# A transformer block on one core: the first layer norm in another order, with x tiles, row sums and scale weights rearranged

## The chip, the cores and the metric

The kernel runs on one core of one Trainium2 chip. The metric is device time in microseconds (us). Every run is of one core. Each run also has the granted clock of the matrix engine, averaged over the run. An average of 1.0 says that no window at a lower clock is on record. Two things escape it. The clock records of these traces begin only at 5.87 to 8.84 us, and the slow warm-up before that (a warm-up every 0.43 us, against 0.22 later) isn't counted. And a trace without any clock record also counts as 1.0.

Names used below: PE is the matrix engine and PEld its weight loads, DVE is VectorE, ACT is ScalarE, POOL is GpSimd, SP is the queue that issues the loads.

## The reference

```python
mod = silu(c) @ w_mod                       # six vectors of 1024: sa, ca, ga, sb, cb, gb
h = layernorm(x) * (1 + ca) + sa            # x: 2048 rows of 1024, bf16
x = x + ga * linear_attention(h)            # h @ wqkv, 32 heads, phi = elu + 1, then @ wo
h = layernorm(x) * (1 + cb) + sb
x = x + gb * swiglu(h)                      # F = 3584
```

Only the first two lines, for the first 512 rows, are touched by the change.

## The kernel before

x stands in tiles of 128 rows (`XRES[:, st, :]`), and four tiles make a chunk. For chunk 0 each tile is normalised, transposed on PE into PSUM (`ps` in the profiles, where its matmuls write), multiplied by the scale column `1 + ca` on its way to `HT`, and used by the first q matmuls. The scale and shift columns come from `w_mod`: `WCA` holds its scale part and `WSA` its shift part, and `mod_sc` makes columns of them with matmuls of one column. PE has nothing real to do before the first tile is normalised, so `warm` gives it matmuls on dummy data.

```python
for st in range(4):
    P.dma("x0_%d" % st, XRES[:, st, :], xv[:, st, :])
...
ca_load(0)            # scale columns 0-511, 1 MB
wq_load(0, 2)
ca_load(1)            # scale columns 512-1023
wq_load(2, 2)
wq_load(4, 2)
sa_load(1)            # shift columns 512-1023
wq_load(6)
wq_load(7)
sa_load(0)            # shift columns 0-511
... # (cut)
act_stats(2)                             # ACT: sum and sum of squares of tile 2
warm(13, bank=3)
s0_[0](); s0_[1](); s1_[0](); s0_[2]()   # DVE: bn_stats of tiles 0, 1; one statement a line in the kernel
ln1_rstd1(0)                             # POOL: (var + eps) ** -0.5
s1_[1](); s1_[2]()
ln1_rstd1(1)
ln1_xn(0)                                # DVE normalises tile 0
tile_transposes(0)
warm(5, bank=3)
s3_[0]()
ln1_xn_act(1)                            # ACT normalises tile 1
tile_transposes(1)
... # (cut: tile 2's mean and variance from ACT's sums, tile 3's bn_stats)
ln1_xn(2)
ln1_xn(3)
mod_sc(WCA, 8, range(2))
fin_ca(0, 2)
tile_transposes(2, 3)
h0_first(0, "dve")                       # PSUM * scale -> HT, then the first q matmuls
... # (cut)
# q phase, in PE's order: q parts dt 0, 1 | mod_sc(WCA, 4..7) | dt 2, 3 | dt 4 |
#   mod_sc(WSA, 6..7) | dt 4, 5 | ... | mod_sc(WSA, 0..3), the last shift columns | dt 7
```

Of the kernel before, what the change touches and what calls it, by code (L numbers as in the profile page):

```python
# [9 lines left out]
ALU = mybir.AluOpType  # L10
# [252 lines left out]
def bass_adaLN_cond__linear_attn_block__swiglu_ffn__prompt_kernel(  # L263
# [12 lines left out]
    S, D = A_x.shape[1], A_x.shape[2]  # L276
# [9 lines left out]
    with ExitStack() as es:  # L286
# [6 lines left out]
        def T(name, off, shape, dt):  # L293
            n = 1
            for s_ in shape[1:]:
                n *= s_
            assert off % 32 == 0 and off + n * mybir.dt.size(dt) <= ARENA, (name, off, shape)
            return nc.alloc_sbuf_tensor_at(name, shape, dt, offset=base + off)

        KB = 1024  # L300
        XRES = T("xres", 0, [128, NST, D], BF16)
        PQT = T("pqt", 32 * KB, [128, NHG, S], BF16)
        WCA = T("wca", 32 * KB, [128, NDT, D], BF16)
# [12 lines left out]
        MV = T("mv", SM + 1632, [128, NST, 2], FP32)  # L316
        VE = T("ve", SM + 1760, [128, NST], FP32)
        RSTD = T("rstd", SM + 1824, [128, NST], FP32)
        NEGHALF = T("neghalf", SM + 1888, [128, 4], FP32)
        SUMX = T("sumx", SM + 1920, [128, NST], FP32)  # L320
        SUMSQ = T("sumsq", SM + 1984, [128, NST], FP32)
# [68 lines left out]
        wmv = w_mod.rearrange("(kt p) n -> p kt n", p=128)  # L390
        cv8 = c.rearrange("o (kt p) -> (o kt) p", p=128)

        P = _Prog()

        P.dma("c", CS8[0:NDT, :], cv8, queue="act")
        for st in range(4):
            P.dma("x0_%d" % st, XRES[:, st, :], xv[:, st, :])

        def ca_load(p):
            P.dma("wca%d" % p, WCA[:, :, 512 * p:512 * p + 512], wmv[:, :, D + 512 * p:D + 512 * p + 512])  # L400

        def sa_load(p):
            P.dma("wsa%d" % p, WSA[:, :, 512 * p:512 * p + 512], wmv[:, :, 512 * p:512 * p + 512])

        def wq_load(i, n=1):
            P.dma("wq%d" % i, WQK[:, i:i + n, 0:D], wqkvv[:, i:i + n, 0:D])

        ca_load(0)
        wq_load(0, 2)
        ca_load(1)  # L410
        wq_load(2, 2)
        wq_load(4, 2)
        sa_load(1)
        wq_load(6)
# [36 lines left out]
        def warm(n=1, bank=2):  # L451
            for _ in range(n):
                P.pe("matmul", out=PS[:, bank, :], lhsT=IDENT[:], rhs=E1[:, 0, :], start=True, stop=True)
# [6 lines left out]
        def ln1_stats_ops(st):  # L460
            par, j = (st // 4) % 2, st % 4
            return [
                lambda: P.dve("bn_stats", out=STATS[:, par, j, 0, :], in_=XRES[:, st, 0:512]),
                lambda: P.dve("bn_stats", out=STATS[:, par, j, 1, :], in_=XRES[:, st, 512:1024]),
                lambda: P.dve("bn_aggr", out=MV[:, st, :], in_=STATS[:, par, j, :, :]),
            ]
# [10 lines left out]
        def ln1_xn(st):  # L477
            P.dve("tensor_scalar", out=XRES[:, st, :], in0=XRES[:, st, :],
                  scalar1=MV[:, st, 0:1], scalar2=RSTD[:, st:st + 1], op0=ALU.subtract, op1=ALU.mult)
# [22 lines left out]
        def mod_sc(w, c0, ms):  # L502
            for m in ms:
                for kt in range(NDT):
                    P.pe("matmul", out=PS[:, 0, c0 + m:c0 + m + 1], lhsT=w[:, kt, m * 128:(m + 1) * 128],
                         rhs=SILUC[:, kt:kt + 1], start=mod_first[0], stop=(kt == NDT - 1), skip_group_check=True)
                    mod_first[0] = False

        def fin_ca(m, n):
            P.dve("tensor_scalar", out=MODCOL[:, 0, m:m + n], in0=PS[:, 0, 8 + m:8 + m + n], scalar1=1.0, scalar2=None,  # L510
                  op0=ALU.add)
# [26 lines left out]
        def h0_first(dt, eng):  # L538
            if eng == "act":
                P.act("activation", out=HT[:, 0, dt, :], in_=t_view(dt), func=ACT.Copy, scale=MODCOL[:, 0, dt:dt + 1])  # L540
            else:
                P.dve("tensor_scalar", out=HT[:, 0, dt, :], in0=t_view(dt), scalar1=MODCOL[:, 0, dt:dt + 1],
                      scalar2=None, op0=ALU.mult)
# [12 lines left out]
        def ln1_rstd1(st):  # L556
            P.dve("tensor_scalar", out=VE[:, st:st + 1], in0=MV[:, st, 1:2], scalar1=EPS, scalar2=None, op0=ALU.add)
            P.pool("tensor_tensor", out=RSTD[:, st:st + 1], in0=VE[:, st:st + 1], in1=NEGHALF[:, 0:1], op=ALU.pow)

        def ln1_xn_act(st):  # L560
            P.dve("tensor_scalar", out=NMR[:, st:st + 1], in0=MV[:, st, 0:1], scalar1=RSTD[:, st:st + 1],
                  scalar2=-1.0, op0=ALU.mult, op1=ALU.mult)
            P.act("activation", out=XRES[:, st, :], in_=XRES[:, st, :],
                  func=ACT.Identity, scale=RSTD[:, st:st + 1], bias=NMR[:, st:st + 1])

        def ln1_rstd2(st):
            P.dve("tensor_scalar", out=VE[:, st:st + 2], in0=MV[:, st:st + 2, 1], scalar1=EPS, scalar2=None, op0=ALU.add)
            P.pool("tensor_tensor", out=RSTD[:, st:st + 2], in0=VE[:, st:st + 2], in1=NEGHALF[:, 0:2], op=ALU.pow)
# [3 lines left out]
        def act_stats(st, c0=0, mid=None):  # L572
            n = (D - c0) // 512
            junk0 = HT[:, 1, 0:2, :] if st < 8 else JUNK1
            for fn_, sc_, acc_ in ((ACT.Identity, 1.0 / D, SUMX), (ACT.Square, D ** -0.5, SUMSQ)):
                P.act("activation", out=junk0[:, 0:n, :], in_=XRES[:, st, c0:D].rearrange("p (a b) -> p a b", a=n),
                      func=fn_, scale=sc_, accum_out=acc_[:, st:st + 1])
                if mid is not None:
                    mid()
                    mid = None  # L580

        def act_mv_ops(st):
            return [
                lambda: P.dve("tensor_copy", out=MV[:, st, 0:1], in_=SUMX[:, st:st + 1]),
                lambda: P.dve("scalar_tensor_tensor", out=MV[:, st, 1:2], in0=SUMX[:, st:st + 1],
                              scalar=SUMX[:, st:st + 1], in1=SUMSQ[:, st:st + 1], op0=ALU.mult, op1=ALU.subtract),
            ]

        def neg_rstd(st):
            P.dve("tensor_scalar", out=VE[:, st:st + 1], in0=MV[:, st, 1:2], scalar1=-1.0, scalar2=EPS, op0=ALU.mult,  # L590
                  op1=ALU.add)
            P.pool("tensor_tensor", out=RSTD[:, st:st + 1], in0=VE[:, st:st + 1], in1=NEGHALF[:, 0:1], op=ALU.pow)

        act_stats(2)
        s0_, s1_, s3_ = ln1_stats_ops(0), ln1_stats_ops(1), ln1_stats_ops(3)
        m2 = act_mv_ops(2)

        def tile_transposes(*js):
            for dt in range(NDT):
                for j in js:  # L600
                    c = (dt % 2) * 512 + j * 128
                    P.pe("transpose", out=PSB[:, 4 + dt // 2, c:c + 128], in_=XRES[:, j, dt * 128:(dt + 1) * 128],
                         identity=IDENT[:])

        warm(13, bank=3)
        s0_[0]()
        s0_[1]()
        s1_[0]()
        s0_[2]()
        ln1_rstd1(0)  # L610
        s1_[1]()
        s1_[2]()
        ln1_rstd1(1)
        ln1_xn(0)
        tile_transposes(0)
        warm(5, bank=3)
        s3_[0]()
        ln1_xn_act(1)
        tile_transposes(1)
        warm(0, bank=3)  # L620
        m2[1]()
        m2[0]()
        neg_rstd(2)
        s3_[1]()
        s3_[2]()
        ln1_rstd1(3)
        ln1_xn(2)
        ln1_xn(3)
        mod_sc(WCA, 8, range(2))
        fin_ca(0, 2)  # L630
        tile_transposes(2, 3)
        h0_first(0, "dve")
        h0_first(1, "dve")
        raw_copy(4, "dve")
# [456 lines left out]
        for ch in range(NCH):  # L1091
# [34 lines left out]
            for j in range(4):  # L1126
                st = 4 * ch + j
# [61 lines left out]
```

## Time and profile before

| | before |
|---|---|
| time, median of 3 runs | 831.27 us (831.02 to 831.39) |
| profiled span | 829.4 us |
| PE busy | 824.2 us |
| first q matmul starts | 11.87 us |

The page of the profiled run, its first lines: busy time of each engine, with the share of the span.

```profile
span 829.4 us, 10016 instructions
PE 824.2 (99%) x4083; PEld 379.2 (46%) x4083; DVE 310.3 (37%) x665; ACT 196.3 (24%) x335; POOL 40.7 (5%) x58
```

PE is busy nearly all the time. Where it is not, the chain of waits tells. Columns: start, length, engine and tile (us).

```profile
0.79 2.74 DMA xres<-in_A_x_dram
...
3.55 1.88 DVE stats L176 x3
...
9.36 0.79 POOL rstd L176
...
10.17 0.56 DVE xres L176
...
10.78 1.01 PE ps L176 x15
...
11.87 114.85 PE ps L176 x673
...
145.30 0.76 DVE g L176
...
146.11 680.82 PE ps L176 x3229
...
826.95 0.30 DVE ut L176
```

Up to 11.87 us the chain is the norm; from there it is PE, but for a side path (cut here) that ends at 146.11, where PE waits for the z row (sums for the attention that go out to DRAM and come back). The timeline of the first 12 us (start, length, engine, instruction, count, and in brackets the idle time before it and what ended it):

```profile
2.61 5.62 PE L176 MATMUL ps<-e,ident 128*128 128x512 bf16 x13 [0.22 <-DVE e L176]
...
5.40 1.06 ACT L176 ACTIVATE ht<-xres 128x1024 bf16<-128x1024 bf16 x1 [2.53 <-DMA xres<-in_A_x_dram]
...
8.06 0.61 PE L176 MATMUL ps<-ident,xres 128*128 128x128 bf16 x8
...
8.51 1.24 PE L176 MATMUL ps<-e,ident 128*128 128x512 bf16 x5
...
9.59 0.61 PE L176 MATMUL ps<-ident,xres 128*128 128x128 bf16 x8
...
11.84 0.56 PEld L176 LDWEIGHTS ps<-ht,wqk 128*128 128x128 bf16 x4 [0.22 <-issue]
...
20.62 0.67 PEld L176 LDWEIGHTS ps<-siluc,wsa 128*128 128x128 bf16 x16
...
24.95 1.07 PEld L176 LDWEIGHTS ps<-siluc,wsa 128*128 128x128 bf16 x32
```

What to see: the 13 warm-ups run right into the first transposes (8.06), five more fill the time to the next (9.59), ACT stands idle until the third x tile lands (5.40), and the shift weights (`wsa`) are used at 20.62 and 24.95 without a wait. From issue and time to landing they land at 20.50 and 24.87, so there is 0.1 us to spare.

The stretches view, for the start and for three kinds of load. Columns: stretch and its length, busy time of PE, PEld, DVE, ACT and POOL with instruction counts, granted clock, DMA share, GB/s.

```profile
7.98:11.39 3.41, 3.29 (x50) 2.48 (x49) 2.45 (x10) 1.24 (x1) 1.33 (x2) 1.00 1.08 368
6.20:9.00 2.80, 2.80 (x17) 1.30 (x15) 2.70 (x11) 2.44 (x5) 1.60 (x3) 1.00 1.07 378
13.90:15.10 1.20, 1.20 (x8) 0.52 (x6) 0.54 (x2) 0.46 (x2) 0.00 (x0) 1.00 1.05 385
233.00:243.00 10.00, 10.00 (x48) 4.50 (x46) 4.79 (x17) 3.45 (x6) 4.72 (x6) 1.00 1.20 291
```

In all four the DMA share is over 1 (1.05 to 1.20). The last stretch is a burst of FFN weights in runs of 512 bytes (5678 of its 5770 packets), at 291 GB/s. The two before it carry runs of mostly 1 KB (693 of 882 packets, 378 GB/s) and of 2 KB (201 of 264, 385 GB/s).

### The profile page before, as it was taken

The numbers are of one execution on the slowest core, as the hardware profiler recorded it, in microseconds if no ns is written. First come the engines' busy times: TensorE is split into PE (matmuls) and PEld (weight loads), VectorE is DVE, ScalarE is ACT, GpSimd is POOL, SyncE is SP. The second block draws the span as 40 slices with busy tenths as digits, with TensorE's granted clock in tenths as the row PEclk, the third lists the DMA queues.
The fourth block names the chain that finished last, engine by engine and source line by source line (L and its number), as shares of the span: only waits on it lengthen the run. The fifth ranks groups of instructions, "written<-read, shape, count | busy, mean of one in ns | idle before, by whom it ended". The sixth has DMA issues, their size and how long they took to land.

```text
span 829.4 us, 10016 instructions
## 1 busy us (share of the span) xinstructions
PE 824.2 (99%) x4083; PEld 379.2 (46%) x4083; DVE 310.3 (37%) x665; ACT 196.3 (24%) x335; POOL 40.7 (5%) x58
## 2 busy tenths in 40 slices
PE   8999999999999999999999999999999999999998
PEld 4544444444444444444444444444444444444444
DVE  5797986666955521111221111122111111111111
ACT  3757641323242111011111101111110111111011
POOL 1010000000130000030000003000000300000000
PEclk9999999999999999999999999999999999999999
DMA  9969655938397985700455571045557004553000
GB/s 324 283 151 230 151 158 172 191 113 304 59 258 226 290 255 154 194 25 13 125 151 152 153 188 31 14 125 153 153 150 193 26 17 123 153 152 89 0 26 26
DMA packets 199246, 119.29 MB, mean 144 GB/s; under 512 B 57880, under 2 KB 182944, under 8 KB 199200
## 3 DMA queue, kind: packets, MB, share of 16 engines
q1 hardware_dynamic: 199184, 118.65, 52.7%
q8 instruction: 32, 0.52, 0.3%
q14 instruction: 14, 0.11, 0.0%
q10 hardware_dynamic: 16, 0.00, 0.0%
HBM read 100.67 MB, written 4.33 MB: 127 GB/s over the span
## 4 chain that ended last, share of the span: by engine, by line
PE 96%; DMA 2%; DVE 1%; SPq 0%; ACT 0%; issue 0%; POOL 0%; ACTq 0%
PE ps L176 96%; DMA z_row<-zr 1%; DMA zb<-z_row 0%; DVE stats L176 0%; DMA xres<-in_A_x_dram 0%; DVE mhl L176 0%; SPq L176 0%; DVE xres L176 0%; DVE pqt L176 0%; POOL rstd L176 0%; DVE g L176 0%; DVE mv L176 0%; ACT gtmp L176 0%; ACT e L176 0%; DVE ve L176 0%
## 5 line engine op out<-in xcount | busy, mean ns | idle before, releaser
L176 PE MATMUL ps<-h2t,gug 128*128 128x512 bf16 x896 | 211.7, 379 | 0.0
L176 PE MATMUL ps<-h2t,guu 128*128 128x512 bf16 x896 | 211.7, 379 | 0.0
L176 DVE TENSOR_TENSOR at<-sg,ps 128x512 bf16<-128x512 bf16 x112 | 77.0, 687 | 284.8 <-PE ps L176 283.2
L176 ACT ACTIVATE sg<-ps 128x512 bf16<-128x512 f32 x112 | 66.9, 597 | 309.7 <-PE ps L176 309.7
L176 PEld LDWEIGHTS ps<-h2t,guu 128*128 128x128 bf16 x896 | 87.7, 98 | 105.7
L176 PEld LDWEIGHTS ps<-h2t,gug 128*128 128x128 bf16 x896 | 87.6, 98 | 105.5
L176 PE MATMUL ps<-wd_a,at 128*128 128x512 bf16 (+2 forms) x528 | 113.5, 373 | 0.0
L176 PE MATMUL ps<-ht,wqk 128*128 128x512 bf16 x512 | 111.8, 379 | 0.1
L176 PE MATMUL ps<-wd_b,at 128*128 128x512 bf16 (+2 forms) x396 | 85.8, 373 | 0.0
L176 PEld LDWEIGHTS ps<-wd_a,at 128*128 128x128 bf16 x528 | 51.1, 98 | 59.8
L176 DVE TENSOR_TENSOR ut<-att,gb_b 128x512 bf16<-128x512 bf16 (+1 forms) x32 | 13.5, 421 | 167.7 <-ACT att L176 167.7
L176 PEld LDWEIGHTS ps<-ht,wqk 128*128 128x128 bf16 x512 | 49.4, 98 | 58.7 <-DVE ht L176 0.4
L176 ACT ACTIVATE att<-ps 128x512 bf16<-128x512 f32 (+1 forms) x32 | 17.4, 591 | 182.1 <-PE ps L176 182.1
L176 PEld LDWEIGHTS ps<-wd_b,at 128*128 128x128 bf16 x396 | 38.3, 98 | 44.7
L176 PE MATMUL ps<-pk,xres 128*128 128x512 bf16 x256 | 56.7, 379 | 0.1
L176 PE MATMUL ps<-mw,pqt 128*128 128x512 bf16 x256 | 56.3, 379 | 0.0
L176 POOL TENSOR_SCALAR h2t<-h2t,modcol 128x512 bf16<-128x512 bf16 x32 | 26.4, 841 | 383.1 <-DMA h2t<-xn 383.1
L176 ACT ACTIVATE e<-ps 128x512 bf16<-128x512 f32 x56 | 33.1, 603 | 31.8 <-PE ps L176 19.6
L176 PEld LDWEIGHTS ps<-mw,pqt 128*128 128x128 bf16 x256 | 24.9, 98 | 30.2 <-DVE xres L176 0.4
L176 PEld LDWEIGHTS ps<-pk,xres 128*128 128x128 bf16 x256 | 24.8, 98 | 30.3 <-DVE g L176 0.6
L176 ACT ACTIVATE junk<-xres 128x1024 bf16<-128x1024 bf16 x24 | 25.4, 1058 | 35.1 <-DVE xres L176 34.9
L176 DVE SCALAR_TENSOR_TENSOR xres<-ps,xres 128x512 bf16<-128x512 f32 x32 | 21.4, 688 | 12.3 <-PE ps L176 11.5
(102 smaller groups left out, 341.1 us busy)
## 6 DMA issues: line engine op xcount, KB each, us to landing
gug<-in_B_w_gate_dram SPq DMA_DIRECT2D x56, 512.0 KB, 4.0
guu<-in_B_w_up_dram SPq DMA_DIRECT2D x56, 512.0 KB, 5.3
xres<-in_A_x_dram SPq DMA_DIRECT2D x20, 256.0 KB, 7.7
rb<-recip_den SPq DMA_DIRECT2D x8, 512.0 KB, 12.1
stgx<-in_w_mod_dram SPq DMA_DIRECT2D x2, 2048.0 KB, 7.9
wd_a<-in_B_w_down_dram SPq DMA_DIRECT2D x4, 1024.0 KB, 7.4
out_dram<-xres SPq DMA_DIRECT2D x31, 128.0 KB, 1.7
xres<-in_A_x_dram SPq DMA_DIRECT2D x3, 1024.0 KB, 14.2
```

What stands on the lines that cost most here:

```text
L176: return getattr(e, method)(**kw)
```

## The change

Its intent is to use ACT, which stood idle for its x tile. Tile 2 is loaded first; ACT takes the sums of tiles 2 and 3 and normalises tile 0; DVE normalises 1, 2 and 3. The first half of the scale weights comes in two pieces of 256 columns, so that the first scale columns are ready sooner, and the second half moves behind one more pair of q weights. PE's 5 warm-ups between tiles become 2, at another place.

```diff
-        for st in range(4):
+        for st in (2, 0, 1, 3):
             P.dma("x0_%d" % st, XRES[:, st, :], xv[:, st, :])
...
-        ca_load(0)
+        ca_load(0, 256)
         wq_load(0, 2)
-        ca_load(1)
+        ca_load(256, 512)
         wq_load(2, 2)
+        ca_load(512, 1024)
         wq_load(4, 2)
...
         warm(13, bank=3)
-        s0_[0]()
-        s0_[1]()
-        s1_[0]()
-        s0_[2]()
-        ln1_rstd1(0)
...
-        ln1_xn(0)
-        tile_transposes(0)
-        warm(5, bank=3)
-        s3_[0]()
-        ln1_xn_act(1)
-        tile_transposes(1)
...
-        ln1_xn(2)
-        ln1_xn(3)
-        mod_sc(WCA, 8, range(2))
-        fin_ca(0, 2)
-        tile_transposes(2, 3)
+        act_stats(2)
+        act_stats(3)
+        s0_, s1_ = ln1_stats_ops(0), ln1_stats_ops(1)
+        for f in (s0_[0], s0_[1], s1_[0], s1_[1], s0_[2], s1_[2]):
+            f()
+        ln1_rstd2(0)
+        act_var(2)
+        ln1_xn_act(0)
+        ln1_xn(1)
+        tile_transposes(1)
+        mod_sc(WCA, 8, range(2))
+        act_var(3)
+        act_xn(2, 0, D)
+        fin_ca(0, 2)
+        warm(2, bank=3)
+        tile_transposes(2)
+        tile_transposes(0)
+        act_xn(3, 0, 512)
+        act_xn(3, 512, D)
+        tile_transposes(3)
         h0_first(0, "dve")
```

(Cuts are marked by three dots; `act_stats(2)` stood further up before. `act_var` and `act_xn` are small new helpers. One GpSimd power of two columns replaces two of one, so GpSimd has one instruction fewer, 57 against 58 on the page.)

More of the change, by code (lines that the diff above doesn't have):

```diff
@@ L395, in bass_adaLN_cond__linear_attn_block__swiglu_ffn__prompt_kernel, with ca_load @@
         P.dma("c", CS8[0:NDT, :], cv8, queue="act")
-        for st in range(4):
+        for st in (2, 0, 1, 3):
             P.dma("x0_%d" % st, XRES[:, st, :], xv[:, st, :])
-        def ca_load(p):
-            P.dma("wca%d" % p, WCA[:, :, 512 * p:512 * p + 512], wmv[:, :, D + 512 * p:D + 512 * p + 512])
+        def ca_load(c0, c1):
+            P.dma("wca%d" % c0, WCA[:, :, c0:c1], wmv[:, :, D + c0:D + c1])
         def sa_load(p):
@@ L592, in neg_rstd @@
             P.pool("tensor_tensor", out=RSTD[:, st:st + 1], in0=VE[:, st:st + 1], in1=NEGHALF[:, 0:1], op=ALU.pow)
-        act_stats(2)
-        s0_, s1_, s3_ = ln1_stats_ops(0), ln1_stats_ops(1), ln1_stats_ops(3)
-        m2 = act_mv_ops(2)
         def tile_transposes(*js):
@@ L603, in tile_transposes, with act_var, act_xn @@
                          identity=IDENT[:])
-        warm(13, bank=3)
-        s0_[0]()
-        s0_[1]()
-        s1_[0]()
-        s0_[2]()
-        ln1_rstd1(0)
-        s1_[1]()
-        s1_[2]()
-        ln1_rstd1(1)
-        ln1_xn(0)
-        tile_transposes(0)
-        warm(5, bank=3)
-        s3_[0]()
-        ln1_xn_act(1)
-        tile_transposes(1)
-        warm(0, bank=3)
-        m2[1]()
-        m2[0]()
-        neg_rstd(2)
-        s3_[1]()
-        s3_[2]()
-        ln1_rstd1(3)
-        ln1_xn(2)
-        ln1_xn(3)
-        mod_sc(WCA, 8, range(2))
-        fin_ca(0, 2)
-        tile_transposes(2, 3)
+        def act_var(st):
+            P.dve("scalar_tensor_tensor", out=MV[:, st, 1:2], in0=SUMX[:, st:st + 1], scalar=SUMX[:, st:st + 1],
+                  in1=SUMSQ[:, st:st + 1], op0=ALU.mult, op1=ALU.subtract)
+            neg_rstd(st)
+        def act_xn(st, c0, c1):
+            P.dve("tensor_scalar", out=XRES[:, st, c0:c1], in0=XRES[:, st, c0:c1],
+                  scalar1=SUMX[:, st:st + 1], scalar2=RSTD[:, st:st + 1], op0=ALU.subtract, op1=ALU.mult)
+        warm(13, bank=3)
+        act_stats(2)
[14 more added lines that the diff above has]
+        tile_transposes(2)
+        tile_transposes(0)
+        act_xn(3, 0, 512)
+        act_xn(3, 512, D)
+        tile_transposes(3)
         h0_first(0, "dve")
```

## The prediction

> **What bounds it now.** The table of busy times gives PE 99% of an 829.4 us span; the chain of waits is 96% PE matmuls. The stretch PE does not own is the start: the chain runs from x tile 0's load (3.53 us) through DVE statistics, POOL rstd and DVE normalisation to the first q matmul at 11.87 us. After that PE is all but gapless (timeline: 22 matmuls start between 16.09 and 20.84, 216 ns each). Only the first 12 us can shrink, and only if nothing later holds PE back.
>
> **What holds it back.** In the first 30 us the DMA page shows the engines at 9 in nearly every slice, some 350 GB/s: one saturated queue, in order. Issue plus time to landing, against first use in the timeline:
> - scale weights wca, second half: 13.45, used 15.07
> - shift weights wsa, first loaded: 20.50, used 20.62
> - wsa, last loaded: 24.87, used 24.95
>
> The last two have 0.1 us of slack, so an earlier first matmul can hardly gain more.
>
> **What the change does.**
> 1. Start. ACT idled 2.53 us for x tile 2; now it lands first and ACT sums tiles 2 and 3, 1.18 us a pass, four passes. Tile 3 lands at 6.1, so its sums end near 8.5 and ACT normalises tile 0 (1.24 us) until 9.8. DVE has four bn_stats (0.62 us) instead of six; tile 1 is normalised near 8.7, tile 2 near 9.7, tile 3 near 10.6. PE then has 24 transposes (56 ns each), 16 small matmuls and 2 warm-ups; the first q matmul falls at 11.6 to 12.1.
> 2. Loads. Half of wca comes in 256-column pieces: 512 B runs instead of 1 KB. In this trace 512 KB of FFN weights, also 512 B runs, take 1.81 us in the saturated burst at 232 to 244 us; 1 MB in 1 KB runs takes 2.97. Two pieces cost 2 x (1.81 - 1.49) = 0.64 us, and all behind them lands that much later. [...] this trace shows 512 B below 1 KB, and decides.
> 3. Order. wca's last 512 columns now follow the second q weight pair: 13.45 + 1.37 + 0.64 = 15.4, against use at 15.1: a new PE wait of 0.3 us.
> 4. wsa then lands near 21.1 and 25.5, PE waits, and that fixes the shift: about +0.5 us by 27 us, whatever the start gained. Later chains start from PE's position and move along.
>
> **Predicted:** 831.7 us, range 830.8 to 832.6. Faster by over 2%: 0.005; within 2%: 0.985; slower: 0.01.
>
> **Signs.** Right: first q matmul within 0.3 us of 11.87; PE or weight-load waits at wca's last part and at wsa; wsa landing 0.4 to 0.8 us later; ACT's wait for x gone; everything from 30 us on shifted by one constant. Wrong: wsa landings unchanged, or a first matmul near 11 us and PE gapless after.
>
> **What would make it wrong.** (a) wsa's landing trails on one slow engine (first share 18.13, last 20.50, after a 16 KB instruction fetch at 16.25); should the fetch fall elsewhere, wsa comes up to 1.4 us earlier and a gain can stay. (b) Five warm-ups become two. [...] before, cold warm-ups took 427 ns and warm matmuls 216. Cold first q matmuls would cost 1 to 2 us more.

About 0.5 us (item 4) on the 831.27 us of before come to 831.8, predicted as 831.7.

## The result, and the profile after

| | before | changed |
|---|---|---|
| median of 6 runs each | 831.26 us | 833.36 us |
| range | 831.02 to 832.30 | 832.24 to 834.12 |
| runs with clock 1.0 | | 832.24, 832.47 |
| runs with clock 0.998 | | 833.36, 833.36, 833.39, 834.12 |
| profiled span | 829.4 us | 831.6 us (clock 0.998) |

The ratio of the changed kernel to the one before is 1.0021, with a 95% interval of 1.0008 to 1.0034. Such ratios are the mean time of one kernel's runs over that of the other's of the same rounds, so not quite the ratio of the medians quoted. Under the 2% rule the change is "same"; it is slower by a small amount that is clear of noise. The predicted range ended at 832.6; the median lies 0.8 us above it, and of the six runs only the two at clock 1.0 lie inside.

The page, the chain of waits and the timeline after, with the same columns as before:

```profile
span 831.6 us, 10012 instructions
PE 823.8 (99%) x4080; PEld 379.7 (46%) x4080; DVE 309.8 (37%) x662; ACT 198.6 (24%) x339; POOL 40.5 (5%) x57
```

```profile
7.76 0.72 POOL rstd L176
...
8.72 0.47 DVE xres L176
...
9.23 4.05 PE ps L176 x46
13.28 0.49 DVE ht L176
...
13.90 814.80 PE ps L176 x4016
...
828.72 0.30 DVE ut L176
```

```profile
2.61 4.58 PE L176 MATMUL ps<-e,ident 128*128 128x512 bf16 x13 [0.22 <-DVE e L176]
...
5.87 1.29 DVE L176 BATCH_NORM_STATS2 stats<-xres 128x6 f32<-128x512 bf16 x2 [0.24 <-DMA xres<-in_A_x_dram]
...
9.23 1.02 PE L176 MATMUL ps<-ident,xres 128*128 128x128 bf16 x8 [2.05 <-DVE xres L176]
...
10.51 1.01 PE L176 MATMUL ps<-e,ident 128*128 128x512 bf16 x2
...
11.32 2.17 PE L176 MATMUL ps<-ident,xres 128*128 128x128 bf16 x24
...
13.87 0.56 PEld L176 LDWEIGHTS ps<-ht,wqk 128*128 128x128 bf16 x4 [0.56 <-issue]
```

The first normalised tile now comes at 9.2 us instead of 7.2. The 13 warm-ups end at 7.19, so PE idles for 2.05 us. About half of this gap is chance: the same 13 warm-ups took 4.58 us here and 5.62 in the kernel before, 1.04 us more, and 4.58 to 5.73 over all profiles with 13. They came every 0.43 us until just before the first clock record (full clock, from 5.87 us here and from 7.98 there), and every 0.22 us from 5.94 us on here. After that the 8 transposes take 1.02 us instead of 0.61, and two warm-ups take 1.01 us, against 0.59 in e3 below: PE is slow. The stretches view shows why:

```profile
5.87:9.28 3.41, 1.36 (x7) 0.45 (x6) 2.75 (x10) 2.65 (x6) 1.45 (x2) 1.00 1.10 348
9.28:12.70 3.42, 3.42 (x39) 2.87 (x40) 1.44 (x6) 0.80 (x1) 0.79 (x1) 0.50 1.11 344
```

From 9.28 to 12.70 us, 3.41 us, the granted clock was 0.50 (half of 3.41 is 0.2% of the span; 0.996 is what two such windows would give). In the window before it PE was busy for 1.36 us of 3.41. In the kernel before, the window from 7.98 had 3.29 us busy and the clock stayed up. The chain of waits agrees: 4.05 us of PE, the transposes, stand between the norm and the first scale multiplication.

So the first q matmul starts at 13.90 instead of 11.87, 2.03 us later. The last DVE step of the kernel comes 1.77 us later (828.72 against 826.95): the rest is absorbed at 146 us, where PE no longer waits for the z row (its matmuls there start 0.46 us apart before, and at most 0.23 us now). The span grew by 2.13 us (831.57 against 829.44 with one digit more than the page prints), so 0.36 us more is lost at the very end.

### The profile page after: what moved, and what is told of

The parts are those of the page before. It is cut to its first block, busy times and chain, and to the rows that moved or that the text cites. A ratio compares the mean times of both kernels' runs of the same rounds, so it can differ in the third digit from the quotient of the medians. Undisturbed runs are those within 1.5% of the kernel's fastest.

```text
span 831.6 us, 10012 instructions
## 1 busy us (share of the span) xinstructions
PE 823.8 (99%) x4080; PEld 379.7 (46%) x4080; DVE 309.8 (37%) x662; ACT 198.6 (24%) x339; POOL 40.5 (5%) x57
## 4 chain that ended last, share of the span: by engine, by line
PE 98%; DMA 0%; DVE 0%; SPq 0%; POOL 0%; issue 0%
PE ps L176 98%; DMA xres<-in_A_x_dram 0%; DVE stats L176 0%; SPq L176 0%; POOL rstd L176 0%; DVE xres L176 0%; DVE ht L176 0%; DVE mv L176 0%; DVE ut L176 0%; DVE nmr L176 0%; DVE ve L176 0%
```

## The experiments

Theories:

1. Clock: the idle gap before the first transposes costs a window at half clock.
2. PE's queue: the late warm-ups and the 24 transposes behind the last norms lengthen the start even at full clock.
3. Loads: 512-byte runs delay everything behind them, and PE waits for it.
4. GpSimd's program has a length that makes the end of the kernel slow.

The rival to all of them is that the norm itself is late and nothing else matters. The kernel before ran beside them: medians 831.31 in the first call, 831.27 in the second (the same chip, the first call's runs shared), 831.64 in the third, 831.35 in the fourth. The third call ran on another chip and the fourth on yet another, so times are compared within a call where possible. In each call one to three of its runs reach 832.1 to 832.5. Against that scatter a handful of runs tells little: of the kernels below only b1, e4 and f4 have an interval of the ratio that lies wholly above 1 (a1 and a2 just reach it); where a smaller difference of times is quoted, it is not clear of noise by itself, and the profiles have to decide. In the edits the changed line of the helper `ca_load`, which now takes column bounds, is left out.

What a wait costs PE is read from the starts of its matmuls, 216 ns apart when nothing holds them: in c2 below weight loads waited 0.6 us in all while the matmuls before them still ran, the matmuls still started 216 and 217 ns apart, and nothing was lost.

To compare starts between profiles, the tables below use two marks of the timeline: the start of the instruction that the third x tile to land releases, and the first q weight load. Some records of matmuls are missing in some traces, weight loads were not at this place.

### First call: one part after another taken out of the changed kernel, and the loads alone

`a1_warm18`:

```diff
-        warm(13, bank=3)
+        warm(18, bank=3)
```

> The changed kernel with 18 instead of 13 warm-up matmuls ahead of its first transposes, so that PE's idle gap before the transposes of tile 1 (2.05 us in the profile) shrinks to about 1 us. Theory 1 (the gap makes the clock drop to half for one window of 3.41 us, which costs about half of the loss): clock 1.0 in every run, first q matmul at 12.5 to 12.8 us instead of 13.90, time 832.2 to 832.5, as in the two runs of the changed kernel that had clock 1.0. Rival (the clock only happens to be lower and costs nothing, the late norm sets the start): first q matmul still later than 13.5 and 833.2 or more.

Measured: 832.27 us median (832.53, 832.27, 832.13, 833.35, 831.94), clock 1.0 in all five. The first q weights load at 13.07, later than expected, but here the third x tile was also late (6.54 instead of 5.87). The clock part of theory 1 holds: no run is noted below 1.0 (why one took 833.35 is not known), and the median is 1.1 us below the changed kernel's. The window of its profile from 7.64 us on has PE busy for 2.65 us of 3.41, and the clock stayed up:

```profile
7.64:11.05 3.41, 2.65 (x33) 1.53 (x32) 2.40 (x12) 3.07 (x5) 2.23 (x3) 1.00 1.12 343
```

`a2_warm18_nowarm2`, the same and:

```diff
-        warm(2, bank=3)
```

> As the kernel with 18 warm-ups, and the 2 warm-ups between the scale matmuls and the transposes of tile 2 taken out. Theory 2 (PE itself is the last wait of the start, with 24 transposes queued behind the last norms): first q matmul 0.3 to 0.45 us earlier than with them. If the loads set the floor (theory 3), the time then falls only to about 831.9 to 832.0 and PE waits at the shift weights, which land at about 21.25; if they do not, it falls to about 831.8.

Measured: 832.39 us (832.08 to 833.12). In the profile the first q weights load at 11.91, 6.17 us after the third tile, where it was 6.53: earlier by 0.36 us, as expected. PE then stands at the last scale piece and at the shift weights (landed at 15.71 and 21.59, used at 15.76 and 21.63), which costs its matmuls 0.40 and 0.31 us. The times did not fall.

`a3_oldpieces`, the same and the old loads:

```diff
-        ca_load(0, 256)
+        ca_load(0, 512)
         wq_load(0, 2)
-        ca_load(256, 512)
+        ca_load(512, 1024)
         wq_load(2, 2)
-        ca_load(512, 1024)
         wq_load(4, 2)
```

> As the kernel before this one in the list, with the scale weights loaded in two pieces of 512 columns in the old order. Theory 3 (256-column pieces cost about 0.65 us of load time, which all later loads inherit): the shift weights land 0.5 to 0.7 us earlier, at about 20.5 to 20.7 and 24.9 to 25.1, and the time falls by 0.1 to 0.4 us to about 831.5 to 831.8. If the 512-byte runs cost nothing: landings and time the same within 0.15 us.

Measured: 832.46 us (831.68 to 832.62). The shift weights land at 19.96 and 24.34 and nothing waits for them, but the time misses the expectation by 0.7 us. Something that none of the three theories names was left. Part is chance (third x tile at 6.34). The other part is at the end: in the trace's semaphore records, which the views leave out, GpSimd's last step comes 0.41 to 0.43 us after the one before it in the changed kernel and in all three of these, and 0.08 us in the kernel before. Hence theory 4.

`b1_pieces`, the kernel before with only the new loads:

```diff
-        ca_load(0)
+        ca_load(0, 256)
         wq_load(0, 2)
-        ca_load(1)
+        ca_load(256, 512)
         wq_load(2, 2)
+        ca_load(512, 1024)
         wq_load(4, 2)
```

> The kernel before with only the load change: scale weights in pieces of 256, 256 and 512 columns, the last behind the second pair of q weights. Theory 3: shift weights land 0.5 to 0.8 us later than in the kernel before (20.50 and 24.87), PE waits for them, and the time is 831.6 to 831.95, 0.4 to 0.7 us over before. If the loads had slack after all or the runs cost nothing: 831.1 to 831.4.

Measured: 832.72 us (832.15 to 833.30; the last of these had clock 0.998), 1.4 us over before, twice what was expected. The profile shows a third x tile at 6.39 and first q weights at 12.76, so the start was late for a reason other than the pieces; the pieces themselves held its matmuls up for 0.19 us, at the last scale piece.

### Second call: the kernel before again, and its loads one by one

`c0_before_again`: no edit.

> The kernel before, unchanged: a null test and a second profile of it. Expected 831.0 to 831.5. What is asked of the profile: whether the late last shares of x (third tile 6.3 to 6.5, fourth 7.0 to 7.3 in three of the last profiles, against 5.37 and 6.10 in the profile of before) are chance, in which case they may show here too and the first q matmul moves with them, or belong to the changed kernels, in which case this one shows 5.2 to 5.5 and 6.0 to 6.2 and a first q matmul at 11.8 to 11.9.

Measured: 832.15, 831.26, 831.02, 831.38 us, median 831.32. The profiled run happened to be the slowest, 832.15, and it answers the question:

```profile
6.71 1.06 ACT L176 ACTIVATE ht<-xres 128x1024 bf16<-128x1024 bf16 x1 [3.84 <-DMA xres<-in_A_x_dram]
...
13.08 0.56 PEld L176 LDWEIGHTS ps<-ht,wqk 128*128 128x128 bf16 x4 [0.22 <-issue]
```

In the unchanged kernel, too, the third tile can land 1.3 us later (6.71 against 5.40), and the first q matmul moves with it (13.08 against 11.84). This is chance, and it is as large as the effects looked for. The shift weights, too, land a microsecond later here than in the first profile (21.53 and 25.90). Single profiles must therefore be compared from the third tile on.

`c2_runs512`, short runs alone:

```diff
-        ca_load(0)
+        ca_load(0, 256)
+        ca_load(256, 512)
         wq_load(0, 2)
-        ca_load(1)
+        ca_load(512, 1024)
```

> The kernel before, the first 512 columns of scale weights as two loads of 256 columns, one after the other, everything else in the old order: 512-byte runs alone. If short runs cost load time (0.30 us each 512 KB): the shift weights land about 0.6 us later than in the unchanged kernel of this call, and the time is 0.4 to 0.7 us over it. If they do not: same landings within 0.2 us, same time within 0.2 us.

Measured: 831.38, 832.27, 831.79, 831.88 us, median 831.84, 0.57 over before, but the ratio's interval is 0.9991 to 1.0022. The shift weights land at 20.93 and 25.31, 0.43 and 0.44 later than in the first profile of before, and PE's weight loads wait for them, which they did not before (waits of the weight loads, 12 to 40 us: total, times, longest; then the matmuls that use them):

```profile
PEld ps L176 <- DMA wsa<-in_w_mod_dram: 0.6, 2, 0.3
...
21.03 0.54 PE L176 MATMUL ps<-siluc,wsa 128*128 128x1 bf16 x16
...
25.36 0.95 PE L176 MATMUL ps<-siluc,wsa 128*128 128x1 bf16 x32
```

The matmuls, though, show no idle time there: they start 216 and 217 ns after the ones before, as everywhere. The waits are hidden behind running matmuls and cost nothing in this profile. So c2 does not show that PE pays for short runs; that they delay the loads behind them is shown by all 18 profiles together (under item 2 below).

`c3_order`, order alone:

```diff
         wq_load(0, 2)
-        ca_load(1)
         wq_load(2, 2)
+        ca_load(512, 1024)
         wq_load(4, 2)
```

> The kernel before, with 512-column pieces, but the second scale piece behind the second pair of q weights: order alone. Theory: it lands about 14.8 against a first use at 15.07, so nothing waits and the time is that of the unchanged kernel within 0.2 us. Rival (the order is what costs in the kernel with pieces): a wait of PE at 15 us and 0.4 us or more.

Measured: 831.41, 831.56, 831.12, 833.07 us, median 831.49. Without the last run, whose cause was not looked at, this is the time of before: the order alone costs nothing that these runs can show.

`c4_xorder`:

```diff
-        for st in range(4):
+        for st in (2, 0, 1, 3):
```

> The kernel before, only the x tiles in the order third, first, second, fourth. VectorE works on the first and second tile, which now land 0.6 and 1.2 us later, ScalarE gets the third 1.8 us earlier. VectorE's chain leads the start in the kernel before, so the first q matmul should come 0.4 to 0.7 us later and the time be 831.6 to 832.0. If ScalarE's sums lead the start: earlier first q matmul and no loss.

Measured: 832.18 us median (831.81 to 832.40). First q weights at 12.46, 0.62 us later, as expected of DVE's chain; the median is 0.2 us over the expected range. With the old norm the new x order brought no gain; that it hurts is not clear of noise (interval 0.9995 to 1.0022).

### Third call: the end, the mended kernel, the dose of warm-ups

`e1_a3_pool`, `a3_oldpieces` with one idle memset more:

```diff
         P.pool("memset", ap=NEGHALF[:], constant=-0.5)
+        P.pool("memset", ap=NEGHALF[:], constant=-0.5)
```

> The new norm order with every suspected cost taken out: 18 warm-ups, none between the scale matmuls and the transposes, 512-column pieces in the old order, and one more (idle) memset on GpSimd, so that GpSimd again runs as many instructions as in the kernel before. Theory 4: the four profiles of the changed kind show GpSimd's last instruction about 0.35 us later and two 8 KB instruction fetches at the very end, none of the six others does; the count brings that about. Expected: no fetch at the end, the last GpSimd step 0.08 us after the one before it, and the time 0.3 to 0.4 us under the kernel without the memset (832.46 median), about 831.5 to 832.1. Rival (it has another cause): same end, same time.

Measured: 831.32 us median (831.17, 831.27, 831.93, 831.32, 831.86) beside 831.64 of before; ratio 0.9997, interval 0.9983 to 1.0010; profiled span 829.4, that of before. GpSimd's last step is back at 0.08 us. One 8 KB fetch was still seen at the end (at 828.64), so the fetches that the theory spoke of are not what marks the slow end. This mended kernel keeps the new norm order and is level with the kernel before. It is 2 us under the changed one, and by these runs not shown to be faster than before.

`e2_before_pool69`:

```diff
-        P.pool("memset", ap=NEGHALF[:], constant=-0.5)
+        P.dve("memset", ap=NEGHALF[:], constant=-0.5)
```

> The kernel before with its one constant memset (0.10 us, at 1.3 us) moved from GpSimd to VectorE: the reverse test of theory 4. Expected: the instruction fetches at the end appear, GpSimd's last step comes 0.4 us after the one before it, and the time is 0.3 to 0.4 us over before, 831.5 to 831.7. Rival: same end, same time as before within 0.15 us.

Measured: 832.00 us median, 0.36 over before: the expected number, but not for the expected reason. The last step came after 0.08 us. The edit had taken two records off GpSimd (68, not 69). In its profile the shift weights landed at 21.54, a microsecond later than in before, and its matmuls stood for 0.59 us, with the old pieces. But the excess of the five runs (831.87 to 832.36) lies elsewhere: their time exceeds the profiled span by 2.17 to 2.26 us, where it is 1.68 to 1.85 in every other run told here, and the median of their spans is 829.8 against 829.9 of before in this call. So the 0.4 us lie outside the span; their cause is open.

`e3_after_pool`, the changed kernel with only that memset:

```diff
         P.pool("memset", ap=NEGHALF[:], constant=-0.5)
+        P.pool("memset", ap=NEGHALF[:], constant=-0.5)
```

> The changed kernel with only the idle GpSimd memset added. Theory 4: no late fetch, so its runs at full clock 831.8 to 832.1 instead of 832.24 and 832.47, and those at clock 0.998 about 833.0 instead of 833.4; theory 1: the clock still falls in about two runs of three, with a first q matmul at 13.5 or later there. Rival to theory 4: unchanged, 832.2 to 832.5 and 833.3 to 833.4.

Measured: 831.89, 832.22, 831.82, 832.51 us at clock 1.0 and 832.96 at 0.998. Both kinds are lower on average than in the changed kernel, although the kernel before was slower in this call. The clock fell once in five, not in two of three, a difference that so few runs can't settle. The profile fell in a run at full clock, so it shows what the changed kernel does when it keeps its clock (first transposes, then PE's weight loads):

```profile
9.32 0.62 PE L176 MATMUL ps<-ident,xres 128*128 128x128 bf16 x8 [1.89 <-DVE xres L176]
...
12.49 0.56 PEld L176 LDWEIGHTS ps<-ht,wqk 128*128 128x128 bf16 x4 [0.56 <-issue]
...
15.99 0.86 PEld L176 LDWEIGHTS ps<-siluc,wca 128*128 128x128 bf16 x32 [0.38 <-DMA wca<-in_w_mod_dram]
...
21.60 0.47 PEld L176 LDWEIGHTS ps<-siluc,wsa 128*128 128x128 bf16 x16 [0.38 <-DMA wsa<-in_w_mod_dram]
...
25.96 0.86 PEld L176 LDWEIGHTS ps<-siluc,wsa 128*128 128x128 bf16 x32 [0.35 <-DMA wsa<-in_w_mod_dram]
```

The weight loads wait for exactly the three loads that the prediction named; the matmuls are held up by only 0.05, 0.05 and 0.03 us. PE had idled for 1.89 us before the first transposes, and this time it kept its clock. With the clock at half, PE comes later than all three, and no such wait shows.

`e4_warm10`:

```diff
-        warm(13, bank=3)
+        warm(10, bank=3)
```

> The changed kernel with 10 instead of 13 first warm-ups: the dose of theory 1 the other way. The gap before the first transposes grows to 2.2 us or more, so the half-clock window should come in every run (clock 0.998 or less) with the first q matmul at 13.7 or later and 833.3 to 834.5. If the gap has nothing to do with the clock: full clock as often as with 13, and the same times.

Measured: 832.89, 833.57, 833.10, 833.77 us; clock 0.998 in three of four, not in all (the one noted as 1.0 took 833.10, as long as the others, and may lack its record). The third tile landed early in the profiled run, so the gap was only 1.54 us and the first q weights loaded at 12.65, but the clock fell all the same:

```profile
6.90:10.31 3.41, 1.86 (x33) 1.29 (x32) 2.04 (x10) 3.23 (x5) 2.21 (x3) 1.00 1.10 335
10.31:13.72 3.41, 3.30 (x26) 2.43 (x24) 2.21 (x5) 1.09 (x2) 0.03 (x1) 0.50 1.09 357
```

### Fourth call: one cost at a time

`f1_before_pool_plus`, the last reverse test done right (69 records):

```diff
-        P.pool("memset", ap=NEGHALF[:], constant=-0.5)
+        P.dve("memset", ap=NEGHALF[:], constant=-0.5)
+        P.pool("memset", ap=MEAN2[:], constant=0.0)
```

> The kernel before, its constant memset on VectorE as in the last reverse test, plus one idle memset on GpSimd. The last reverse test took two instructions off GpSimd's record (68), not one; this one should leave 69, as in the changed kernel. Theory 4 in its narrower form (it is that very length of GpSimd's program that puts an instruction fetch at its end): two 8 KB fetches at the end, the last GpSimd step about 0.41 us after the one before it instead of 0.08, and 0.3 to 0.4 us over the kernel before. If not: last step 0.08 us, and the end of the changed kernel has another cause.

Measured: 831.74 us median (831.55 to 832.31) beside 831.35, 0.39 over; the last step came after 0.44 us. Its last DVE and PE work is as early as in before, and the span is 829.8. Over all 18 profiles, the last step takes 0.41 to 0.44 us in the six with 69 GpSimd records and 0.08 or 0.09 us in the twelve with 70 or 68. Only one 8 KB fetch came near the end, after the step. So in these profiles the late step goes with 69 records, whichever kernel has them; by what means, is not shown. The cost in time, 0.39 us, fits the step but is not clear of noise by itself (interval 0.9993 to 1.0019).

`f2_pieces_back`, the mended kernel with the new loads:

```diff
-        ca_load(0, 512)
+        ca_load(0, 256)
         wq_load(0, 2)
-        ca_load(512, 1024)
+        ca_load(256, 512)
         wq_load(2, 2)
+        ca_load(512, 1024)
         wq_load(4, 2)
```

> The mended kernel (18 warm-ups, none later, old loads, idle memset), with only the 256-column pieces put back. The loads alone should cost 0.5 to 0.7 us: 0.5 to 0.7 us over the kernel before's 829.4 us span, 831.8 to 832.0 on a chip where the kernel before has 831.3, with PE waiting at the last scale piece (15.7) and at the shift weights (21.5).

Measured: 832.10 us median (831.70 to 832.38); span 830.0, 0.6 over the mended kernel's. PE's weight loads waited 0.62 us for the last scale piece (used at 15.97), which held its matmuls up for 0.29 us, and used the shift weights at 21.32, just after they landed at 21.24, at no cost.

`f3_warm2_back`, the mended kernel with the late warm-ups again:

```diff
         fin_ca(0, 2)
+        warm(2, bank=3)
         tile_transposes(2)
```

> The mended kernel with only the 2 warm-ups before the last three tiles' transposes put back. PE is the last wait there: first q matmul 0.43 us later (two times 216 ns), about 6.6 us after the third x tile has landed instead of 6.15; time 0.2 to 0.45 us over the mended kernel. Rival: hidden behind the norms, no difference.

Measured: 831.98 us median (831.78 to 832.39). First q weights 6.54 us after the third tile, where the mended kernel has 6.10: 0.44 us, as expected. There was no run of the mended kernel in this call, so the time is compared with before alone (0.63 over), and part of that is the late third tile (6.31 in its profile).

`f4_warm13_back`, the mended kernel with 13 first warm-ups again:

```diff
-        warm(18, bank=3)
+        warm(13, bank=3)
```

> The mended kernel with only the first warm-ups back at 13. Theory 1: clock 0.998 in some of the runs (four of six in the changed kernel), and these 0.8 to 1.5 us longer than its own runs at full clock; those at full clock the same as the mended kernel.

Measured: 831.44 and 831.53 us at clock 1.0; 832.36, 832.75 and 833.30 at 0.998; 834.96 at 0.996. The same program falls into two kinds by its clock alone. The mean of the three at 0.998 is 1.3 us over that of the two at 1.0. The profile was taken in one of the runs at half clock. PE's gap before the first transposes was 0.92 us, and one of 0.69 followed:

```profile
7.64:11.05 3.41, 1.80 (x30) 1.13 (x29) 1.59 (x7) 2.34 (x4) 2.23 (x3) 1.00 1.08 379
11.05:14.47 3.42, 2.93 (x26) 2.52 (x25) 2.28 (x6) 0.95 (x1) 0.00 (x0) 0.50 1.09 367
```

### The starts side by side

All from timelines: start of the work that the third x tile releases, and first q weight load.

| kind of start | profiles | third tile to q load, us |
|---|---|---|
| old norm, old x order | before 5.40 to 11.84; again 6.71 to 13.08; c2 5.67 to 12.03; c3 5.81 to 12.16; f1 5.70 to 12.06; b1 6.39 to 12.76; e2 5.55 to 12.00 | 6.35 to 6.45 |
| new norm, 2 late warm-ups, full clock | a1 6.54 to 13.07; e3 5.96 to 12.49; f3 6.31 to 12.85 | 6.53 to 6.54 |
| new norm, none, full clock | a2 5.74 to 11.91; a3 6.34 to 12.47; e1 5.98 to 12.08; f2 6.13 to 12.23 | 6.10 to 6.17 |
| changed kernel, half clock | 5.87 to 13.87 | 8.00 |

Profiles of e4 and f4 are left out, since there the third tile landed while DVE was still busy, and so is c4, a mixture of the kinds. Within a kind the distance is steady to 0.1 us while the landing moves by 1.3 us. This gives the sum for the two profiles:

| term | us | from |
|---|---|---|
| third x tile landed later | +0.47 | 5.40 to 5.87; chance, as far as the runs show |
| half clock | +1.47 | 8.00 - 6.53 |
| two late warm-ups | +0.40 | 6.53 - 6.13 (mean of the four) |
| new norm order by itself | -0.31 | 6.13 - 6.44 |
| first q load | +2.03 | 11.84 to 13.87 |
| taken back at 146 us | -0.26 | 1.77 - 2.03 |
| end of GpSimd and the rest | +0.36 | 2.13 - 1.77; GpSimd's step alone 0.35 |
| span | +2.13 | 829.44 to 831.57 |

The table is subtraction across profiles, and each of its large terms has an experiment of its own: f4 for the clock, f3 for the warm-ups, c0 for the landing, f1 for the end.

## Why the prediction was right or wrong

**What bounds the kernel: right.** After the start nothing but PE matters (98% of the changed kernel's chain, 96% before), and all effects are those of the first 30 us (and, unforeseen, of the last one).

**Item 1, "the first q matmul falls at 11.6 to 12.1": wrong, by the clock.** It came at 13.90. The estimate counted the norm, the transposes at 56 ns and the 2 warm-ups, and assumed full clock and the third tile landing as before. Under those two conditions it was right: 5.40 + 6.53 is 11.93. But it did not ask what PE does while it waits. With the first normalised tile 2 us later and the 13 warm-ups unchanged, PE idles (2.05 us in the profile), and in four of six runs a window at half clock followed, worth 1.47 us in the profile and 1.2 us between the means of the four runs and of the other two. This is the step that failed: the two runs at full clock, 832.24 and 832.47, lie inside the range.

**"What would make it wrong", (b): named, but misplaced.** The prediction saw that five warm-ups become two and put a fall of the clock outside its range. It looked for the risk in the late warm-ups. The gap was elsewhere, ahead of the first transposes: 2.05 us in the changed kernel, 1.54 in e4 and 0.92 in f4. What the traces show is this. The half clock lasted 3.41 us. In the 3.41 us before it PE was busy, as the profile counts it, for 1.36 us (the changed kernel), 1.80 (f4) and 1.86 (e4); every other window of this length at the start, counted on from the first clock record of the 14 traces that have one, had 2.65 (a1) or more and was followed by full clock. None lies in between. The longest gap doesn't order the runs: f4 lost the clock with 0.92 us, e3 kept it with 1.89. The windows with so little work began at 5.87, 6.90 and 7.64 us, in three kernels, and the same program lost the clock in some runs and kept it in others (the changed kernel in four of six).

**Item 2, short runs delay the loads by 0.64 us: right in kind, near in size.** The shift weights landed at 21.25 and 25.61 in the changed kernel, 0.75 and 0.74 us later than before, and 0.43 later with the short runs alone (c2). One pair of profiles proves little here, as c0 shows: 21.53 in the unchanged kernel. But each load lands in 16 shares, and the first share of the first shift load came at 18.13 to 18.66 us in all ten profiles with the old pieces and at 18.93 to 19.09 in all eight with the new ones, 0.57 us between the means. The case (a) under "what would make it wrong" did not come: the shift weights still trailed by 2.27 us from first to last share. The trace of before has 291 GB/s with 512-byte runs and 378 to 385 with longer ones.

**Items 3 and 4, new waits at the last scale piece and at the shift weights "whatever the start gained": right only where the start is near the old one.** a2, whose first q weights load at 11.91, lost 0.40 us at the last scale piece and 0.31 and 0.03 at the shift weights; from its first q load to the last weight load of the matmuls on `modtmp`, near 28 us, it took 0.77 us longer than the 15.53 of before. f2 (start 12.23) lost 0.30 on the same stretch and e3 (12.49) 0.16, so it is not "whatever the start gained". How late the loads land by chance counts as well: e2 lost 0.63 with the old pieces. In the profile on record nothing is lost (15.53): PE was 2 us late and the loads had landed. So here the floor set by the loads and the late start did not add.

**"Everything from 30 us on shifted by one constant": wrong in two places.** At 146 us a wait of before took back 0.26 us, and at the end GpSimd added about 0.35 us, which no step of the prediction could have found in the profile before: its last step took 0.43 us with 69 records, against 0.08 with 70 before.

**The signs.** ACT's wait for x did shrink, from 2.53 us to 0.69 for its first tile and 0.73 for its second, and the new norm was worth something: the new order by itself starts q 0.31 us sooner after the third tile. It was lost to the rest. Of the other signs two came: the shift weights landed 0.4 to 0.8 us later, and in e3, where the clock held, the weight loads waited as named.

**Open.** Why the landing of the third x tile scatters, by 1.3 us in the same program (the new x order does not make it later: it landed at 5.87 us on average in the eleven profiles with that order and in the seven with the old one); why the clock fell in some runs of a program and not in others; how GpSimd's last step comes to be late with 69 records and not with 68 or 70; what e2 loses outside its span.

## What to carry to other kernels

When a change makes the matrix engine wait longer before its first real work, recount its warm-ups. Here 13 of them left a window of 3.41 us with PE busy for 1.36 us (1.80 in f4), and the next one, at half clock, cost 1.47 us in the profile, more than the 0.31 us that the new order gained; with 18 the window had 2.65 us (a1) or 3.03 (e1) and the clock stayed up. When effects of a few tenths of a microsecond are at stake, split the runs by their clock average and compare profiles from a shared event (here the landing of a tile) on, since chance at the start (1.3 us in the landing of one tile) is larger than the effects. Put one cost at a time back into a mended kernel: taking them out one after another from a bad one showed no fall in the times after the first (a1) until the last was gone (e1).
